# Banded attention and a gated MLP in one kernel: the plain units' scores and sink products take all 128 rows of the array

## The chip, the cores and the metric

One core of a Trainium2 chip runs the whole program. The metric is the device time of one execution in microseconds (us), as the median of several runs. TensorE (PE) multiplies, VectorE (DVE), ScalarE (ACT) and GpSimd (POOL) do the elementwise work, SyncE (SP) issues every DMA. PEld in a profile is TensorE's weight load, which may run beside a product.

## The reference, cut to what matters

```
# q, k, v: [4, 8, 768, 64]; n_sink = 4, window = 128 (read on the chip)
scores = q @ k.T / sqrt(64)
keep   = (col < n_sink) | ((row - col >= 0) & (row - col < window))
a      = softmax(where(keep, scores, -1e9))        # sum + 1e-9 below
x      = (a @ v) -> [3072, 512]                    # heads side by side
out    = (sigmoid(x @ w_gate) * (x @ w_val)) @ w_out     # 512 -> 1536 -> 512
```

Everything is float32.

## The kernel before, in words

**Attention.** The work is cut into units: one head of one stretch of T = 2 tiles (256 tokens); there are 96, numbered u, the heads of a stretch in a row. `attend` (line 719) records the steps of a unit: loads of q, k and v; per tile a product of scores (`qk`), mask and row maximum on DVE (`top`), exponential on ACT (`exp`); the sum's inverse (`guard` and a reciprocal) and the scaling of P on POOL, ACT or DVE; transposes of P on TensorE (`turn`), a copy to `wt`, two triangular selections on POOL (`split`), and the products with v (`pv`), the last of which is that of the sinks, the 16 first tokens' columns. A score tile has 144 columns (its own 128 keys and 16 sinks) or 272 (and the 128 keys before).

**Plain units.** The first 16 units (`PLAIN`, line 31) multiply in float32, which takes four times as many passes; the later ones split their operands into two fp32r halves side by side and then contract over all 128 rows anyway. A plain unit holds q and k turned, head dimension on the rows, in `qkT`, of which only rows 0 to 63 are used; its scores therefore contract over K = D = 64 rows (line 760). The sinks' product contracts over 16 rows: the sinks' v in `VSRAW` and their weights, copied out of PSUM into one buffer `low` (line 887; line 888 is the copy), both at rows 0 to 15 for even heads and 64 to 79 for odd ones (line 923). In a trace these are `a<-qkT 64*128` (rows * columns of the loaded weights) and `a<-low,xr 16*64`; `a<-wt,vraw 128*64` are the products with v.

**MLP.** Tokens are taken in nine chunks. Chunk 0 (`WHOLE = 1`, 2 tiles) multiplies float32 weights as they come, as soon as the first eight units have left their results in `X0` (they lie in buffers named `qs`, `kh`, `kl` and `vhl`): `m<-qs,ws` and its like are its up products, `o<-ws,th` its down products. Weights come in 36 loads of 512 KB into three buffers `wst` and are decoded by ACT, POOL and DVE (`decode`, line 1006). Later chunks multiply fp32r halves (`m<-XH,ws`, `m<-XL,ws`, `o<-ws,gh`).

**What sets the order.** Nothing is issued as it is written. Each step is given to a planner (`Plan`, line 256) with a priority, a duration for each engine that can do it, and what it reads and writes. `Plan.run` plays the steps through in a model of time, picks for each engine the ready step of lowest priority, chooses an engine where there are several, gives out buffers, and writes down one fixed order for each engine. At times when TensorE would stand idle in that model, before 130 us, it adds a filler, a product of the identity with itself (`warm`, `m<-ident` in a trace), so that TensorE stays active. The model counts a plain unit's scores as half activity (`busy=0.5`, line 781). All engines then run their fixed orders and wait for each other by semaphores. Since all steps are recorded by one helper, line 489 stands in nearly all rows of the trace.

Of the kernel before, what the change touches and what calls it, by code (L numbers as in the profile page):

```python
# [9 lines left out]
F32 = mybir.dt.float32  # L10
# [10 lines left out]
NS = 16  # L21
# [52 lines left out]
BUFS = {}  # L74
# [157 lines left out]
class Tile:  # L232
# [7 lines left out]
    def __call__(self):  # L240
        if isinstance(self.pool, list):
            return self.pool[self.slot]
        if self.got is None:
            name = f"{self.tag}{self.slot}"
            self.got = self.pool.tile(self.shape, self.dtype, tag=name, name=name, bufs=1)
        return self.got


# [187 lines left out]
def kernel(  # L436
# [17 lines left out]
    B, H, D, S = q.shape  # L454
    DM, DF, _ = w_gate.shape
# [5 lines left out]
    KW = 128 + NS  # L461
# [6 lines left out]
    p1 = main.enter_context(tc.tile_pool(name="p1", bufs=1))  # L468
# [10 lines left out]
    plan = Plan()  # L479

    class InOrder:


        def __init__(self, engine):
            self.engine = engine
# [5 lines left out]
    PE, V, A, G, Q = (  # L491
        InOrder(e) for e in (nc.tensor, nc.vector, nc.scalar, nc.gpsimd, nc.sync)
    )
# [10 lines left out]
    def mac(cols):  # L504
        return max(cols * 13 / 12 / 2.4, 104.5) + 2.5

    def dma(prio, ns, fn, r=(), w=()):
        plan.op(prio, [("Q", 460, fn)], r, w, dma=ns)

    def copy(prio, cols, out, in_, r, w, psum=False):  # L510

        plan.op(
            prio,
            [
                ("A", act(cols, psum), lambda: A.copy(out=out(), in_=in_())),
                ("V", vec(cols, not psum), lambda: V.tensor_copy(out=out(), in_=in_())),
            ],
            r, w,
        )
# [23 lines left out]
    class Fixed:  # L543
# [5 lines left out]
        def __call__(self):  # L549
            return self.tile  # L550

    def tile(shape, dtype, tag, bufs, pool=None):
        return Tile(pool or p1, shape, dtype, tag, bufs)
# [5 lines left out]
    VSRAW = tile([128, H // 2, D], F32, "xr", BUFS["xr"])  # L559
# [115 lines left out]
    chunk_of = [i for i, parts in enumerate(MT) for _ in range(sum(parts))]  # L675
    X0 = {}

    def sinks(b, u):
        if not b:
            for o in (0, 64):  # L680
                dma(
                    u, 91.0, lambda o=o: Q.dma_start(
                        out=VSRAW()[o : o + NS],
                        in_=v[b, o // 64 :: 2, 0:NS, :].rearrange("h p d -> p h d"),
                    ), w=[(VSRAW, o)],
                )
        raw = tile([128, H, D], F32, "wst", BUFS["wst"], p2)
        u = max(u, PLAIN) + SINKP
        for o in range(0, 128, NS):
            dma(  # L690
                u, 91.0, lambda o=o: Q.dma_start(
                    out=raw()[o : o + NS], in_=v[b, :, 0:NS, :].rearrange("h p d -> p h d"),
                ), w=[(raw, o)],
            )
        for i in range(2):
            hs = slice(i * H // 2, i * H // 2 + H // 2)
            x, hi = lambda hs=hs: raw()[:, hs], lambda hs=hs: VSHL()[:, hs, 0:D]
            copy(u, H // 2 * D, hi, x, [raw], [(VSHL, i)])
            rest(u, H // 2 * D, lambda hs=hs: VSHL()[:, hs, D : 2 * D], x, hi, [raw], [(VSHL, i)])

    def load(u, b, h, t0, T, prev, L, vraw, qkT, plain):

        W, k0 = T * 128, (t0 - prev) * 128
        for part, src, o, n in ((0, k, (t0 - prev) * KW, L * KW), (2, q, t0 * 128, W)):
            at = 0 if part else W
            for i in range(1 if plain else 2):
                dma(
                    u, 0.75 * n, lambda i=i, src=src, o=o, n=n, at=at: Q.dma_start(
                        out=qkT()[i * D : i * D + D, at : at + n],
                        in_=src[b, h, :, o : o + n],  # L710
                    ), w=[(qkT, part + 4 * i)],
                )
        dma(
            u, 182.0 * L, lambda: Q.dma_start(
                out=vraw(), in_=v[b, h, k0 : k0 + L * 128].rearrange("(l p) d -> p l d", p=128)
            ), w=[vraw],
        )

    def attend(u, b, h, t0, T, XR):

        prev = 1 if t0 else 0
        L = T + prev
        W = T * 128
# [2 lines left out]
            sinks(b, u)  # L726
        plain = u < PLAIN
        vraw = tile([128, L, D], F32, "vraw", BUFS["vraw"])
        qkT = tile([128, W + L * KW], F32, "qkT", BUFS["turned"])
        qT = lambda: qkT()[:, 0:W]  # L730
        kTf = lambda: qkT()[:, W : W + L * KW]
        load(u, b, h, t0, T, prev, L, vraw, qkT, plain)
        kk2, qq2 = [(qkT, 0), (qkT, 4)], [(qkT, 2), (qkT, 6)]
        if plain:
            pairs = ((qT, kTf),)
            qk_reads, qk_ns = [qkT], 4
        else:
# [10 lines left out]
            pairs = (qs, kh), (qs, kl)  # L748
# [4 lines left out]
        for t in range(T):  # L753
            sc = tile([128, 512], F32, "a", BUFS["a"], ps)
            first = t0 + t == 0
            n = KW if first else KW + 128

            def qk(t=t, sc=sc, n=n):
                s0 = max(t + prev - 1, 0) * KW
                K = D if plain else 128  # L760
                for i, (qq, kk) in enumerate(pairs):
                    PE.matmul(
                        sc()[:, 0:n], lhsT=qq()[0:K, t * 128 : t * 128 + 128],
                        rhs=kk()[0:K, s0 : s0 + n], start=i == 0, stop=i == len(pairs) - 1,
                    )

            def top(t=t, sc=sc, first=first):
                if not first:
                    V.copy_predicated(out=sc()[:, 0:128], mask=tri, data=sc()[:, KW : KW + 128])
                V.tensor_tensor_reduce(  # L770
                    out=P()[:, t], in0=sc()[:, 0:KW], in1=am[min(t0 + t, 2)], op0=ALU.add,
                    op1=ALU.min, scale=-SCALE, scalar=3.0e38, accum_out=negm_all[:, u, t : t + 1],
                )

            def exp(t=t):
                A.activation(
                    out=P()[:, t], in_=P()[:, t], func=AF.Exp, bias=negm_all[:, u, t : t + 1],
                    scale=-1.0, accum_out=rs()[:, t : t + 1],
                )

            plan.op(u, [("PE", 10 + qk_ns * mac(n), qk)], qk_reads, [sc, (P, t)], busy=0.5 if plain else 0.9)
            plan.op(
                u, [("V", 290 if first else 600, top)],
                [sc, (MASKS, 3), (MASKS, min(t0 + t, 2))], [sc, (P, t)],
            )
            plan.op(u, [("A", 460, exp)], [], [(P, t), (rs, t)])
# [28 lines left out]
        if not plain:  # L815
            st = tile([128, T, 2, NS], F32R, "st", BUFS["st"])
            turned = tile([128, T, 2 * NS], F32, "turned", BUFS["st"])
            sk = tile([128, T, 4, 32], F32R, "sk", BUFS["sk"])
# [23 lines left out]
        w = lambda: wt()[:, 0:Z]  # L842
# [41 lines left out]
        o = 64 * (h % 2)  # L884
        if plain:
            vhl = vraw
            sk = tile([128, W], F32, "low", BUFS["small"])
            copy(u, W, lambda: sk()[o : o + NS], lambda: tp()[0:NS, W : 2 * W], [tp], [sk], True)
        else:
            vhl = tile([128, L, 2 * D], F32R, "vhl", BUFS["vhl"])  # L890
            copy(u, L * D, lambda: vhl()[:, :, 0:D], vraw, [vraw], [(vhl, 0)])
            rest(
                u, L * D, lambda: vhl()[:, :, D : 2 * D], vraw, lambda: vhl()[:, :, 0:D],
                [vraw, (vhl, 0)], [(vhl, 1)],
            )
# [9 lines left out]
        for l in range(L):  # L905
            tl = l - prev
            n = 128 if (tl < 0 or tl == T - 1) else 256
# [6 lines left out]
        def pv():  # L914
            a = (xr()[e : e + D] if plain else acc())[:, 0 : Z * W].rearrange("p (z x) -> p z x", z=Z)
            for i, (_, l, c0, r0, n) in enumerate(blocks):
                PE.matmul(
                    a[:, :, c0 : c0 + n], lhsT=vhl()[:, l],
                    rhs=w().rearrange("p z t x y -> p z (t x y)")[:, :, r0 : r0 + n],
                    start=i == 0, stop=False, skip_group_check=True,  # L920
                )
            if plain:
                sv, sw = VSRAW()[o : o + NS, h // 2], sk()[o : o + NS]
            else:
                sv, sw = VSHL()[:, h], sk().rearrange("p t x y -> p (t x y)")
            PE.matmul(
                a[:, 0], lhsT=sv, rhs=sw, start=False, stop=True, skip_group_check=True
            )
# [7 lines left out]
        else:  # L936
            low = tile([D, W], F32, "low", BUFS["small"])
# [32 lines left out]
        if h % 2:  # L970
# [8 lines left out]
            for run in runs:  # L979
# [3 lines left out]
                x = lambda cols=cols: xr()[:, cols]  # L983
# [237 lines left out]
    u = g = fed = ci = 0  # L1221
    for b in range(B):
        t0 = 0
        for T in AT[b]:
# [6 lines left out]
            while ci < len(MT) and fed + sum(MT[ci]) <= g:  # L1231
                feed(ci, fed, MT[ci])
                fed += sum(MT[ci])
                ci += 1
    plan.run(WARM, 245.0, warm)
    wres = {f: [w() if i < 4 else w()[:, 0] for i, w in enumerate(ws)] for f, ws in wres.items()}


# [64 lines left out]
```

## Time and profile before

| | |
|---|---|
| median of 3 runs | 822.87 us (820.37 to 824.41) |
| the profiled execution | 821.27 us |
| its span in the trace | 819.3 us |
| TensorE busy | 801.7 us, 98% |
| VectorE busy | 529.1 us, 65% |
| ScalarE busy | 420.1 us, 51% |
| GpSimd busy | 470.0 us, 57% |
| mean granted TensorE clock | 0.988 of full speed |

The span runs from the first to the last recorded instruction; 2.0 us of the execution lie around it. Busy time is the time covered by an engine's instructions. The granted clock is a share of 2.4 GHz; 0.50 is 1.2 GHz. A stretch with a clock between these two holds both. A float32 product shows as two records ("x2"), since it runs in two halves with a weight load each.

### The profile page before, as it was taken

The page shows a single profiled execution, that of the slowest core. Times are in us where ns is not written, and L with a number is a line of the kernel's source. Part 1 is how long each engine was busy: PE and PEld are TensorE (multiplying, and loading weights), DVE is VectorE, ACT ScalarE, POOL GpSimd, SP SyncE. Part 2 cuts the span into 40 slices and gives each one's busy share as a digit, 9 for nine tenths or more (in the row PEclk, how much of TensorE's full clock was granted, in tenths as well). Part 3 has the DMA queues.
Part 4 walks back from the last instruction along what each step waited for, and adds up shares of the span by engine and source line. Part 5 has one row for each costly group of instructions (what it writes and reads, how often), then busy time and mean ns, then how long its engine had stood idle before and what let it go on. Part 6 is the DMA issues. An engine that isn't in the chain of part 4 may idle for free.

```text
span 819.3 us, 14819 instructions
## 1 busy us (share of the span) xinstructions
PE 801.7 (98%) x4472; PEld 706.3 (86%) x4472; DVE 529.1 (65%) x1659; ACT 420.1 (51%) x1232; POOL 470.0 (57%) x666
## 2 busy tenths in 40 slices
PE   7999999999999999999999999999999999999997
PEld 5666576789999999999899988899899999999996
DVE  4668787988888888786951499956961495111111
ACT  4667777766677777654730377734640373001001
POOL 3467788787777777664851488755751474111111
PEclk7899999999999999999999999999999999999999
DMA  5567796454454553334341243433441141112112
GB/s 166 152 175 231 206 275 205 110 149 126 130 157 119 144 130 94 107 105 116 103 113 40 66 137 86 134 100 97 104 119 38 50 109 27 48 34 88 40 38 68
DMA packets 101013, 92.93 MB, mean 113 GB/s; under 512 B 47680, under 2 KB 82496, under 8 KB 100928
## 3 DMA queue, kind: packets, MB, share of 16 engines
q1 hardware_dynamic: 100928, 91.93, 40.4%
q8 instruction: 38, 0.62, 0.3%
q14 instruction: 47, 0.39, 0.1%
HBM read 82.45 MB, written 9.44 MB: 112 GB/s over the span
## 4 chain that ended last, share of the span: by engine, by line
PE 67%; DVE 8%; POOL 2%; ACT 2%; DMA 1%; issue 1%; SPq 0%; POOLq 0%; DVEq 0%; ACTq 0%
PE m L489 39%; PE o L489 19%; PE a L489 9%; DVE rs L489 1%; DMA qkT<-in_k_dram 1%; DVE P L489 1%; DVE st L489 1%; DVE gl L489 1%; POOL kl L489 1%; DVE xr L489 1%; DVE a L489 1%; ACT P L489 1%; DVE low L489 1%; DVE th L489 0%; POOL wt L489 0%
## 5 line engine op out<-in xcount | busy, mean ns | idle before, releaser
L489 PE MATMUL m<-XH,ws 128*128 128x384 f32 (+1 forms) x1536 | 399.7, 325 | 0.2 <-DVE th L489 0.2
L489 PEld LDWEIGHTS m<-XH,ws 128*128 128x128 f32 x1536 | 273.9, 188 | 2.9 <-DVE th L489 0.4
L489 PE MATMUL m<-XL,ws 128*128 128x384 f32 (+1 forms) x768 | 247.6, 322 | 0.0
L489 DVE SCALAR_TENSOR_TENSOR th<-th,m 128x384 f32<-128x384 f32 (+1 forms) x108 | 54.6, 505 | 193.5 <-PE m L489 190.3
L489 POOL TENSOR_TENSOR gl<-th,gh 128x384 fp32r<-128x384 f32 (+1 forms) x61 | 61.4, 1006 | 188.9 <-DVE gh L489 183.5
L489 ACT ACTIVATE th<-m 128x384 f32<-128x384 f32 (+1 forms) x108 | 49.1, 455 | 222.5 <-PE m L489 221.5
L489 PEld LDWEIGHTS m<-XL,ws 128*128 128x128 f32 x768 | 144.9, 189 | 2.5
L489 POOL TENSOR_SCALAR_AFFINE_SELECT wt<-wt 128x512 fp32r<-128x512 f32 (+3 forms) x192 | 121.1, 631 | 33.4 <-DVE wt L489 13.7
L489 PE MATMUL o<-ws,gh 128*128 128x512 f32 x264 | 106.4, 403 | 0.0
L489 PE MATMUL o<-ws,gl 128*128 128x512 f32 x264 | 104.3, 395 | 0.7 <-DVE gl L489 0.4
L489 PE MATMUL o<-wol,gh 128*128 128x512 f32 x264 | 103.2, 391 | 0.0
L489 ACT ACTIVATE P<-P,negm_all 128x144 f32<-128x144 f32 x192 | 78.9, 411 | 29.5 <-DVE negm_all L489 24.3
L489 DVE CUSTOM_DVE_ANT_0 P<-a,am 128x144 f32<-128x144 f32 x192 | 58.3, 305 | 7.9 <-PE a L489 2.2
L489 PEld LDWEIGHTS o<-ws,gl 128*128 128x128 f32 x264 | 49.5, 188 | 14.6 <-DVE gl L489 1.8
L489 ACT ACTIVATE P<-P,rs 128x144 f32<-128x144 f32 x114 | 44.1, 410 | 22.5 <-DVE rs L489 22.1
L489 PEld LDWEIGHTS o<-wol,gh 128*128 128x128 f32 x264 | 49.7, 188 | 5.7
L489 PEld LDWEIGHTS o<-ws,gh 128*128 128x128 f32 x264 | 49.7, 188 | 5.2
L489 POOL TENSOR_TENSOR qs<-qkT,qs 64x256 fp32r<-64x256 f32 x57 | 44.4, 779 | 16.0 <-issue 4.5
L489 POOL TENSOR_TENSOR kl<-qkT,kh 128x432 fp32r<-128x432 f32 (+1 forms) x45 | 50.1, 1112 | 3.9 <-ACT kh L489 2.0
L489 PE MATMUL a<-wt,vhl 128*128 128x256 f32 (+1 forms) x216 | 49.2, 330 | 0.5 <-POOL wt L489 0.3
L489 DVE COPY_PREDICATED a<-tri,a 128x128 f32<-128x128 int32 x160 | 45.4, 284 | 6.2 <-PE a L489 5.5
L489 PE MATMUL a<-kh,qs 128*128 128x272 f32 (+1 forms) x160 | 46.5, 295 | 1.1 <-DVE wt L489 0.5
(129 smaller groups left out, 1460.2 us busy)
## 6 DMA issues: line engine op xcount, KB each, us to landing
wol<-wol_d SPq DMA_DIRECT2D x96, 256.0 KB, 2.8
qkT<-in_k_dram SPq DMA_DIRECT2D x120, 108.0 KB, 2.7
qkT<-in_q_dram SPq DMA_DIRECT2D x176, 64.0 KB, 2.4
wst<-in_moe_w_gate_dram SPq DMA_DIRECT2D x12, 512.0 KB, 4.4
wst<-in_moe_w_val_dram SPq DMA_DIRECT2D x12, 512.0 KB, 4.1
wst<-in_moe_w_out_dram SPq DMA_DIRECT2D x12, 512.0 KB, 4.6
vraw<-in_v_dram SPq DMA_DIRECT2D x64, 96.0 KB, 2.3
out_dram<-w SPq DMA_DIRECT2D x23, 256.0 KB, 2.3
```

Source lines behind the costliest of these rows:

```text
L489: return lambda *a, **kw: tc.keep_in_program_order(op(*a, **kw))
```

## The change: what it does

Scores and sink products of the plain units now contract over all 128 rows. For that the rows that hold nothing must be zero:

- `qkT` of a plain unit is one of three tiles of fixed size that all 16 units share, by slot (`Shared`); rows 64 to 127 of each are set to zero once, for the first three units. The loads write rows 0 to 63 only, as before.
- `VSRAW` is set to zero as a whole before its two loads.
- The sinks' weights go to two tiles `SK0`, zeroed once, one for even and one for odd heads, in the buffers `sk` that the later units use; before it was the single buffer `low`.
- Each zeroing is a step of the planner, for POOL or DVE, at the priority of its unit.

```diff
+class Shared(Tile):
+    def __init__(self, kept, *args):
+        super().__init__(*args)
+        self.kept = kept
+    def __call__(self):
+        if self.got is None:
+            got = self.kept.get(self.slot)
+            self.got = got if got is not None else super().__call__()
+            self.kept[self.slot] = self.got
+        return self.got
...
+    def zero(prio, tile, ns, ap, part=None):
+        plan.op(
+            prio, [("G", ns, lambda: G.memset(ap(), 0.0)), ("V", ns, lambda: V.memset(ap(), 0.0))],
+            w=[tile if part is None else (tile, part)],
+        )
+    SK0 = [tile([128, 2 * 128], F32, "sk", BUFS["sk"]) for _ in range(2)]
+    HALVES, FIRST = {}, []
     def sinks(b, u):
         if not b:
+            zero(u, VSRAW, 300.0, VSRAW)
+            for x in SK0:
+                zero(u, x, 300.0, x)
...
-        qkT = tile([128, W + L * KW], F32, "qkT", BUFS["turned"])
+        qkT = (
+            Shared(HALVES, p1, [128, 2 * 128 + 3 * KW], F32, "qkT", BUFS["turned"]) if plain
+            else tile([128, W + L * KW], F32, "qkT", BUFS["turned"])
+        )
...
+        if u < BUFS["turned"]:
+            zero(u, qkT, 700.0, lambda: qkT()[D:128], 8)
+            FIRST.append(qkT)
...
-                K = D if plain else 128
                 for i, (qq, kk) in enumerate(pairs):
                     PE.matmul(
-                        sc()[:, 0:n], lhsT=qq()[0:K, t * 128 : t * 128 + 128],
-                        rhs=kk()[0:K, s0 : s0 + n], start=i == 0, stop=i == len(pairs) - 1,
+                        sc()[:, 0:n], lhsT=qq()[:, t * 128 : t * 128 + 128],
+                        rhs=kk()[:, s0 : s0 + n], start=i == 0, stop=i == len(pairs) - 1,
                     )
...
-            sk = tile([128, W], F32, "low", BUFS["small"])
+            sk = SK0[h % 2]
...
-                sv, sw = VSRAW()[o : o + NS, h // 2], sk()[o : o + NS]
+                sv, sw = VSRAW()[:, h // 2], sk()
```

The planner's durations and its `busy=0.5` stand as they were, but with five more buffers' steps and other ready times it writes another order. It differs over the first 1,941 of the 4,431 rows of TensorE's order (equal instructions in a run make one row); after them the two orders are the same, row by row. The fillers are 59 before and 60 now.

On TensorE, behind the scores of the first two units (`a_152` and `a_158` are unit 0's second score tile, `m_91<-ident` the fillers, `a_195` and `a_208` the turned P of unit 0), before and now:

```order
L489 MATMUL a_152<-qkT_114 128x272
L489 MATMUL a_162<-qkT_131 128x144
L489 MATMUL a_169<-qkT_131 128x272
L489 MATMUL m_91<-ident 128x128 x4
L489 MATMUL a_195<-ident,P_154 128x128
```

```order
L504 MATMUL a_158<-qkT_109 128x272
L504 MATMUL a_168<-qkT_120 128x144
L504 MATMUL a_175<-qkT_120 128x272
L504 MATMUL m_91<-ident 128x128 x11
L504 MATMUL a_208<-ident,P_164 128x128
```

Eleven fillers stand where four stood, ahead of unit 0's transposes; what is added here is taken out further on.

On SP, the queue of the loads, ahead of the fourth load of weights (`wst`); before, `qkT` is that of units 3, 4 and, behind the weights, 5; now it is that of units 5 and 6:

```order
L489 DMA qkT_166<-in_k_dram 64x288
L489 DMA qkT_166<-in_q_dram 64x256
L489 DMA qkT_178<-in_k_dram 64x288
L489 DMA qkT_178<-in_q_dram 64x256
L489 DMA wst_227<-in_moe_w_gate_dram 128x4x256
L489 DMA qkT_235<-in_k_dram 64x288
```

```order
L504 DMA qkT_122<-in_k_dram 64x288
L504 DMA qkT_122<-in_q_dram 64x256
L504 DMA qkT_109<-in_k_dram 64x288
L504 DMA qkT_109<-in_q_dram 64x256
L504 DMA wst_266<-in_moe_w_gate_dram 128x4x256
```

The fourth load of weights stood behind the loads of unit 4; now it stands behind those of unit 6, which wait until TensorE has read unit 3's scores out of the same buffer.

## Rows read from the trace of the kernel before

**Rows 1.** The page's first part: busy time of each engine, share of the span, instructions.

```profile
PE 801.7 (98%) x4472; PEld 706.3 (86%) x4472; DVE 529.1 (65%) x1659; ACT 420.1 (51%) x1232; POOL 470.0 (57%) x666
```

**Rows 2.** Busy time of each engine by stretches of the span: the stretch and its length, then each engine's busy us (and instructions), the granted clock, the DMA engines' busy share, GB/s.

```profile
8.50:11.30 2.80, 2.80 (x14) 2.65 (x14) 0.98 (x5) 0.48 (x3) 0.98 (x2) 0.50 0.87 281
...
15.00:28.30 13.30, 12.62 (x40) 7.88 (x39) 5.06 (x18) 6.95 (x19) 6.22 (x9) 0.50 0.59 171
28.30:58.20 29.90, 29.90 (x163) 20.02 (x164) 20.58 (x67) 21.75 (x54) 17.80 (x25) 1.00 0.56 163
58.20:131.20 73.00, 73.00 (x314) 47.80 (x313) 58.06 (x144) 56.72 (x126) 57.24 (x64) 1.00 0.81 231
131.20:165.00 33.80, 30.74 (x159) 23.28 (x158) 31.83 (x73) 24.97 (x64) 28.51 (x33) 1.00 0.52 145
165.00:380.00 215.00, 214.48 (x1400) 201.16 (x1399) 176.76 (x598) 140.58 (x464) 154.89 (x237) 1.00 0.46 123
```

**Rows 3.** The timeline of TensorE from 5 to 31.5 us: start, length, what, records in a run, and idle time before with what ended it. A run takes in the rows of other widths that follow it.

```profile
5.73 0.94 PE L489 MATMUL a<-qkT 64*128 64x144 f32 x4 [0.49 <-DMA qkT<-in_q_dram]
...
8.47 2.07 PE L489 MATMUL m<-ident 128*128 128x128 f32 x8
10.34 1.06 PE L489 MATMUL a<-ident,P 128*128 128x128 f32 x4
11.19 0.55 PE L489 MATMUL m<-ident 128*128 128x128 f32 x2
...
13.84 0.66 PE L489 MATMUL a<-ident,P 128*128 128x128 f32 x4 [1.66 <-POOL P L489]
...
15.92 1.54 PE L489 MATMUL a<-wt,vraw 128*64 128x256 f32 x4 [0.68 <-POOL wt L489]
17.39 1.11 PE L489 MATMUL a<-low,xr 16*64 16x256 f32 x2
18.43 1.22 PE L489 MATMUL m<-ident 128*128 128x128 f32 x4
19.59 1.75 PE L489 MATMUL a<-qkT 64*128 64x144 f32 x4
...
24.93 2.08 PE L489 MATMUL m<-ident 128*128 128x128 f32 x8
...
28.22 1.13 PE L489 MATMUL a<-qkT 64*128 64x144 f32 x4
```

**Rows 4.** The waits of all engines from 15.9 to 28.3 us: who waited for whom, us in total, times, longest.

```profile
POOL rs L489 <- ACT P L489: 5.5, 2, 4.4
ACT qs L489 <- PE a L489: 3.6, 1, 3.6
```

**Rows 5.** The timeline of TensorE from 72.3 to 78.5 us, columns as in rows 3.

```profile
72.44 0.59 PE L489 MATMUL m<-qs,ws 128*128 128x256 f32 x2
72.87 0.59 PE L489 MATMUL m<-kh,ws 128*128 128x256 f32 x2
73.39 1.08 PE L489 MATMUL a<-wt,vraw 128*64 128x256 f32 x6
74.41 0.64 PE L489 MATMUL a<-low,xr 16*64 16x256 f32 x2
74.98 1.18 PE L489 MATMUL a<-qkT 64*128 64x272 f32 x4
76.09 1.98 PE L489 MATMUL o<-ws,th 128*128 128x512 f32 x4
77.91 0.59 PE L489 MATMUL m<-kl,ws 128*128 128x256 f32 x2
```

**Rows 6.** The timeline of TensorE from 64.5 to 69.5 us, columns as in rows 3.

```profile
65.27 1.02 PE L489 MATMUL o<-ws,th 128*128 128x512 f32 x2
66.22 0.72 PE L489 MATMUL a<-qkT 64*128 64x272 f32 x2
66.87 1.13 PE L489 MATMUL o<-ws,th 128*128 128x512 f32 x2
67.84 0.60 PE L489 MATMUL a<-ident,P 128*128 128x128 f32 x4
```

**Rows 7.** TensorE's weight loads in the stretch of rows 6, same columns.

```profile
66.22 0.29 PEld L489 LDWEIGHTS a<-qkT 64*128 64x128 f32 x2 [0.76 <-PE a L489]
```

**Rows 8.** What TensorE waited for from 126 to 166 us, columns as in rows 4.

```profile
PE o L489 <- DVE th L489: 1.6, 2, 1.2
PE a L489 <- POOL kl L489: 0.8, 1, 0.8
```

**Rows 9.** GpSimd's groups of instructions in the first 2.5 us: line, operation, shapes, count, busy us and mean ns, idle time before.

```profile
masks.py:197 POOL MEMSET ident<- 128x128 f32 x1 | 0.2, 205 | 0.3 <-POOLq L1275 0.3
```

**Rows 10.** The timeline of GpSimd from 8.4 to 14 us, columns as in rows 3.

```profile
8.67 0.23 POOL L489 TENSOR_SCALAR rs<-rs 128x2 f32<-128x2 f32 x1 [6.40 <-ACT P L489]
...
13.03 0.75 POOL L489 TENSOR_SCALAR P<-P,rs 128x144 f32<-128x144 f32 x1 [0.30 <-DVE rs L489]
```

**Rows 11.** The timeline of SP's DMA issues in the first 60 us, columns as in rows 3.

```profile
14.99 0.37 SPq L489 DMA_DIRECT2D wst<-in_moe_w_gate_dram  x1
```

**Rows 12.** The timeline of TensorE from 28 to 45 us, columns as in rows 3.

```profile
39.86 0.70 PE L489 MATMUL m<-qs,ws 128*128 128x256 f32 x2
```

**Rows 13.** The timeline of TensorE from 147 to 166 us, columns as in rows 3.

```profile
151.92 0.47 PE L489 MATMUL m<-XH,ws 128*128 128x256 f32 x1
```

More of the change, by code (lines that the diff above doesn't have):

```diff
@@ L1235 @@
     plan.run(WARM, 245.0, warm)
+    assert len({x.slot for x in FIRST}) == BUFS["turned"]
     wres = {f: [w() if i < 4 else w()[:, 0] for i, w in enumerate(ws)] for f, ws in wres.items()}
```

## The prediction

> **What bounds the kernel now.** I read the page's first part first: TensorE is busy for 801.7 us of 819.3, no other engine for more than 65% [rows 1]. So the end comes earlier only where TensorE loses time. Next the table by stretches [rows 2]. From 165 to 380 us TensorE is idle for 0.5 us of 215: what has been gained by 165 us stays. TensorE is without a gap from 28.3 to 131.2 us too. From 131.2 to 165 us it is idle for 3.06 us, while DVE is busy for 31.83 of 33.8: there the others set the pace, and TensorE waits for DVE and POOL [rows 8]. The third thing to see is the clock: 0.50 from 8.5 to 11.3 us and from 15 to 28.3 us, and full from there on.
>
> The timeline of that second stretch [rows 3] shows TensorE working without a gap from 15.92 to 28.22 us, 12.3 us, at half clock: plain products with v, sinks' products over 16 rows, scores over 64 rows, a few fillers. The clock rises only behind the fillers and transposes, all over 128 rows, that stand from 24.93 to 28.22 us. The waits of these microseconds [rows 4] show who suffers: ACT waits 3.6 us for TensorE, and POOL waits 5.5 us for an exponential that comes late for the same reason. In this stretch TensorE's speed sets everyone's.
>
> The last view is TensorE's timeline where the clock is full [rows 5 to 7]. Products over the full array follow each other without loss: 0.43 us from one of 256 columns to the next [rows 5], so 0.46 for 272 columns and 0.86 for 512. A product of scores does not fit in so smoothly: from 65.27 to 67.84 us two products of 512 columns and one of scores take 2.57 us, where 0.86 + 0.46 + 0.86 = 2.18 would do [rows 6]. Its weight load, 64 rows by 128 columns, begins when its product does, after 0.76 us without a load [rows 7]; a load ahead of time would have been hidden.
>
> **What the change removes.** *The clock.* If rows without work keep the clock low, scores over 128 rows and sinks over 128 in place of 16 raise it earlier. The 12.3 us from 15.92 us would be 6.15 at full clock, a gain of at most 6.2; the 2.8 us of the first slow stretch [rows 2] would give 1.4 more. Not all of it can come in: unit 0's products with v still wait for POOL at 15.92 us [rows 3], and behind them each unit passes through ACT, DVE and POOL. The lower end is 0, the clock as it is. I take 5.0, near the upper end, because the others' waits there end on TensorE [rows 4].
>
> The Trainium skill speaks against this term. Its page "TensorE: Matmul & The Clock Gate", Part 1, says that the chip watches how busy the engine has been recently and that sustained matmuls release the clock; rows of the array are not in it, and by it the term would be 0. The trace does not agree with it taken as busy time: 12.3 us without a gap, and the clock rose only at the end of them.
>
> *The place of the scores among full products.* A lone product of scores costs 2.57 - 2.18 = 0.39 us beyond its columns [rows 6]. For a pair: 1.11 us from 74.98 to 76.09 where 0.91 would do, and the two products behind it take 1.82 where 1.72 would, together 0.30 [rows 5]. Over 128 rows a scores' weight load has the shape of those that are hidden. The order now holds 10 lone products and 11 pairs: 10 x 0.39 + 11 x 0.30 = 7.2 us of TensorE's time; the two first pairs stand where TensorE waits for loads (0.49 us ahead of 5.73 [rows 3]), which leaves 6.6. Of these, 4 lone ones and 7 pairs stand ahead of the last filler, 3.7 us, and the rest, 2.9, behind it. I take 1.5 of the first part (between 0 and 3.7), since the fillers show a TensorE that has time there, and 0 of the second (between 0 and 2.9): from 58 us to 165 us a faster TensorE would only meet the others' pace sooner. The sinks' products take 0.57 us where 256 columns need 0.43 [rows 5]; being 64 columns wide they stay outside that shape, and I count nothing (between 0 and 0.14 x 16 = 2.2).
>
> **What it adds.** Six zeroings. The nearest row: POOL sets 128 columns to zero in 0.205 us [rows 9], so 256 columns in some 0.41 and 688 in 1.1. POOL's three take 2.6 us, and it is idle for 6.40 us ahead of 8.67 [rows 10]; they stand there. DVE's three have the same columns and end before unit 2 needs its buffer. The cost is nothing, with POOL's idle time as the cover; without it unit 0's scores would start up to 2.6 us later. Contracting over more rows costs no time: a product over 64 rows takes no less per column than one over 128 [rows 5, 6].
>
> **What it moves.** Eleven fillers stand ahead of unit 0's transposes in place of four. Four take 1.87 us at half clock (8.47 to 10.34), 0.47 each [rows 3]: eleven take 5.2 us at half clock and 2.6 at full. At full clock the transposes start at 11.1 us instead of 10.3, but behind them TensorE waited 1.66 us for unit 1's P anyway [rows 3], which POOL scales at 13.03 [rows 10], so that delay is covered. On SP the fourth load of weights, issued at 14.99 [rows 11], now waits for the loads of unit 6, and with them for unit 3's scores. At full clock these come some 2 us after 14.99; chunk 0 does not need these weights yet. For the rest of the new order I put a loss of 1.0 us in the stretch from 131.2 us, where DVE has 2 us of slack and an earlier TensorE will be idle longer (between -1 and 3).
>
> **The sum.** 821.27 - 5.0 - 1.5 + 1.0 = 815.8 us, made against the profiled execution, which is 1.6 below the median of 822.87. I forecast 816. No change that is under 0.5%, 4.1 us, can be told from none here, so faster means below 818.8 and slower above 827.0.
>
> **The rivals.**
> - *Both terms come in whole.* 6.2 + 1.4 of clock and 6.6 + 2.2 of shapes give up to 16; what the others can follow is less, 9 to 14: 807 to 812. For it: ACT, DVE and POOL are busy for under 75% of the time from 28.3 to 58.2 us [rows 2]. Against: 131 to 165 us, where DVE has no room.
> - *The clock stays.* This is the page's rule: only the shapes are left, 1.5 us, and eleven fillers at half clock take about 1 of it back: 821. For it: nothing shows rows by themselves at work; the fillers at 24.93 us are 128 columns wide as well, and the products with v stay at 64. Against: the gapless stretch at half clock.
> - *The others hold the pace.* The clock rises, but ACT, DVE, POOL and the loads arrive at 165 us when they did before, and TensorE's idle time from 131 us grows by what it gained: 820. For it: DVE's 31.83 of 33.8 us. Against: before 58 us they wait for TensorE.
> - *Slower: the weights start late.* The clock stays, and the eleven fillers end at 8.47 + 5.2 = 13.6 us. Up to unit 3's scores, which the fourth load of weights now waits for, stand two units' transposes (0.85 each, 10.34 to 11.19), two pairs of scores (1.75 each [rows 3]) and three fillers (1.4): 20.2 us, and with unit 6's loads 21. That is 6 us behind 14.99 [rows 11], and the next load is behind unit 1's product with v. If chunk 0 ends on its last weights, 5 of these 6 us may arrive at the end: 826 on the profiled execution, 828 on the median. It decides only if the loads have no slack; the DMA share of 0.56 from 28.3 to 58.2 us [rows 2] says that they have some.
>
> **How the numbers follow.** The forecast, 812 to 818.8, has 0.45; both terms whole 0.14; the clock stays 0.18; the others hold the pace 0.14; slower 0.09. Faster: 0.45 + 0.14 = 0.59. Slower 0.09. The rest, 0.32, is within 0.5%. The range, 807.5 to 823.5, holds the first four cases and leaves out the slower one and the tail of the whole gain. The likeliest case alone is 812 to 818.8.
>
> **What would show it.** Right, step by step: a granted clock of 1.00 from about 11 us on, no stretch at 0.50 from 15 to 28; a lone product of scores that takes 0.46 us between its neighbours, with its load ahead of it; the first chunk products (39.86 us before [rows 12]) some 8 us earlier, and the first of chunk 1 (151.92 us [rows 13]) 5 to 6 us earlier; TensorE's idle time from 131 us at 3 to 5 us. I am wrong in the main step if the clock still stands at 0.50 after 16 us; in the place of the gain if the clock is up and chunk 1 opens less than 3 us earlier; and in the zeroings if unit 0's scores start more than 0.3 us after 5.73 [rows 3].

## The result, and the profile after

The changed kernel takes 808.99 us (median of 4 runs, 807.40 to 810.34), the kernel before 822.81 beside it (820.37 to 824.41): ratio 0.9834, 95% interval 0.9803 to 0.9864. That is 13.8 us less, where 6.9 were forecast: direction and range held, the size did not. The profiled execution took 808.61 us, its span is 806.9.

The page's first part, which answers to [rows 1]:

```profile
PE 788.8 (98%) x4474; PEld 705.8 (87%) x4474; DVE 534.9 (66%) x1666; ACT 420.9 (52%) x1233; POOL 475.5 (59%) x664
```

TensorE is busy for 12.9 us less and the span is 12.4 shorter; its idle time is 18.1 us where it was 17.6. So the net gain is busy time of TensorE. The same stretches as in [rows 2], same columns:

```profile
8.50:11.30 2.80, 2.80 (x28) 2.76 (x27) 1.16 (x6) 0.97 (x5) 0.98 (x2) 1.00 0.93 274
11.30:15.00 3.70, 1.26 (x10) 0.99 (x8) 2.05 (x7) 1.96 (x4) 1.90 (x2) 1.00 1.05 311
15.00:28.30 13.30, 12.45 (x59) 8.56 (x60) 7.80 (x27) 7.23 (x20) 6.37 (x12) 0.74 0.43 120
28.30:58.20 29.90, 28.73 (x168) 21.77 (x167) 26.28 (x72) 24.00 (x61) 23.21 (x28) 1.00 0.71 205
58.20:131.20 73.00, 71.03 (x314) 49.81 (x313) 62.15 (x146) 58.64 (x123) 58.98 (x65) 1.00 0.85 243
131.20:165.00 33.80, 33.11 (x207) 28.52 (x206) 30.07 (x83) 26.32 (x74) 29.00 (x34) 1.00 0.52 141
```

Three things: the first slow stretch is gone (1.00 at 8.5 us), of the second about half is left (0.74), and from 131.2 us, where I expected 3 to 5 us of idle time in place of 3.06, TensorE is idle for 0.69. TensorE's timeline from 8 us on, columns as in rows 3, shows where the clock still falls, and the first chunk products:

```profile
8.36 2.62 PE L504 MATMUL m<-ident 128*128 128x128 f32 x22
10.81 0.60 PE L504 MATMUL a<-ident,P 128*128 128x128 f32 x4
...
15.36 0.66 PE L504 MATMUL a<-ident,P 128*128 128x128 f32 x4 [2.80 <-POOL P L504]
...
16.59 1.73 PE L504 MATMUL a<-qkT 128*128 128x144 f32 x4 [0.34 <-DMA qkT<-in_q_dram]
18.24 1.54 PE L504 MATMUL a<-wt,vraw 128*64 128x256 f32 x4
...
22.63 0.77 PE L504 MATMUL a<-sk,xr 128*64 128x256 f32 x2
23.33 1.16 PE L504 MATMUL m<-ident 128*128 128x128 f32 x8
...
32.03 0.60 PE L504 MATMUL m<-qs,ws 128*128 128x256 f32 x2
```

The eleven fillers take 2.62 us for 22 records, full speed. At 12.56 us TensorE runs dry and waits 2.80 us for unit 1's P. Behind that wait the scores of two tiles take 1.73 us, about the half-speed length of [rows 3] (1.75); the fillers of 23.33 us run at full speed again. The first chunk product starts 7.8 us earlier than [rows 12]. A lone product of scores, and then its weight loads, where [rows 6, 7] showed the old shape:

```profile
55.80 0.59 PE L504 MATMUL a<-sk,xr 128*64 128x256 f32 x2
56.32 0.66 PE L504 MATMUL a<-ident,P 128*128 128x128 f32 x4
56.81 1.02 PE L504 MATMUL o<-ws,th 128*128 128x512 f32 x2
57.67 0.62 PE L504 MATMUL a<-qkT 128*128 128x272 f32 x2
58.13 1.02 PE L504 MATMUL o<-ws,th 128*128 128x512 f32 x2
```

```profile
57.25 0.19 PEld L504 LDWEIGHTS a<-qkT 128*128 128x128 f32 x1 [0.24 <-PE a L504]
57.68 0.19 PEld L504 LDWEIGHTS a<-qkT 128*128 128x128 f32 x1 [0.24 <-issue]
```

From the product of scores to its neighbour are 0.46 us, from the neighbour before to it 0.86: the columns alone, no loss. The load at 57.25 runs ahead of its product. The sinks' products start 0.52 us ahead of the next work (0.57 before). The first product of chunk 1, which answers to [rows 13], is 13.9 us earlier. The end is 12.4 earlier: behind this product TensorE is busy for 659.60 us where it was 657.40, as a little work moved there.

```profile
138.02 0.47 PE L504 MATMUL m<-XH,ws 128*128 128x256 f32 x1
```

Between the first chunk product and this one lie 105.99 us, before 112.06 ([rows 12, 13]). The forecast had the first 8 us and the second 5 to 6 us earlier, and so would have lengthened this stretch; it became 6.1 us shorter.

### The profile page after: what moved, and what is told of

The parts are those of the page before. It is cut to its first block, busy times and chain, and to the rows that moved or that the text cites. A ratio compares the mean times of both kernels' runs of the same rounds, so it can differ in the third digit from the quotient of the medians.

```text
span 806.9 us, 14812 instructions
## 1 busy us (share of the span) xinstructions
PE 788.8 (98%) x4474; PEld 705.8 (87%) x4474; DVE 534.9 (66%) x1666; ACT 420.9 (52%) x1233; POOL 475.5 (59%) x664
## 4 chain that ended last, share of the span: by engine, by line
PE 68%; DVE 12%; DMA 5%; POOL 4%; ACT 3%; issue 2%; SPq 1%; POOLq 0%; DVEq 0%; ACTq 0%
PE m L504 39%; PE o L504 20%; PE a L504 9%; DMA wst<-in_moe_w_out_dram 3%; DVE ws L504 2%; DVE rs L504 1%; DMA wst<-in_moe_w_gate_dram 1%; DVE P L504 1%; ACT ws L504 1%; POOL wst L504 1%; DVE xr L504 1%; DVE gl L504 1%; DVE st L504 1%; POOL wt L504 1%; DVE a L504 1%
## 5 line engine op out<-in xcount | busy, mean ns | idle before, releaser
L504 POOL TENSOR_TENSOR gl<-th,gh 128x384 fp32r<-128x384 f32 (+1 forms) x58 | 57.3, 987 | 188.1 <-DVE gh L504 184.7
L504 POOL TENSOR_TENSOR qs<-qkT,qs 64x256 fp32r<-64x256 f32 x61 | 48.6, 797 | 17.7 <-POOL wt L504 5.4
L504 ACT ACTIVATE P<-P,rs 128x144 f32<-128x144 f32 x125 | 47.3, 409 | 21.5 <-DVE rs L504 19.8
L504 POOL TENSOR_TENSOR kl<-qkT,kh 128x432 fp32r<-128x432 f32 (+1 forms) x49 | 54.7, 1117 | 5.2 <-DVE st L504 1.9
```

What stands on the lines that cost most here:

```text
L504: return lambda *a, **kw: tc.keep_in_program_order(op(*a, **kw))
```

## The experiments

The kernel before ran beside each batch: 822.31, 822.67 and 821.57 us (medians). The reader should follow two numbers for each kernel: the time, and how long TensorE works at half speed ahead of 30 us.

**Which part lifts the clock? Four kernels with part of the change.** First the new order and zeroings with the old rows:

```diff
-                        sc()[:, 0:n], lhsT=qq()[:, t * 128 : t * 128 + 128],
+                        sc()[:, 0:n], lhsT=qq()[0:D, t * 128 : t * 128 + 128],
...
-                sv, sw = VSRAW()[:, h // 2], sk()
+                sv, sw = VSRAW()[o : o + NS, h // 2], sk()[o : o + NS]
```

> The changed kernel's order and zeroing, but scores over 64 rows and sinks' products over 16 again, in all plain units. Theory A (the rows themselves bring the gain: clock and the fit of the products on TensorE): about the kernel before, 820 to 825 us, with a clock of 0.50 again over some 13 us between 15 and 30 us and 0.39 us lost around each lone product of scores. Rival R1 (the new order of the planner brings a large part of it): 811 to 816 us.

Measured 812.90 us (6 runs, 809.04 to 824.15), ratio 0.9898 (0.9856 to 0.9939). Theory A, that the rows bring the whole gain, fell here: with no row added, 9.4 us are gone by the medians, 5 to 12 by the interval. Its windows, columns as above, and the fillers:

```profile
11.30:15.00 3.70, 3.70 (x21) 3.43 (x19) 0.65 (x3) 1.34 (x2) 2.22 (x2) 0.56 0.94 297
15.00:28.30 13.30, 13.30 (x75) 8.85 (x74) 10.33 (x38) 9.77 (x26) 7.86 (x13) 1.00 0.50 134
```

```profile
9.01 5.06 PE L504 MATMUL m<-ident 128*128 128x128 f32 x22
```

The eleven fillers run at half speed (5.06 us), but the clock is up from some 14.4 us on and stays. Its runs scatter, though: the longest two, 818.99 and 824.15 us, have mean clocks of 0.991 and 0.983, the shortest 0.999. Without the longest, which the ratio leaves out, the median is 811.80.

Then the reverse, the order of before with all rows:

```diff
-                K = D if plain else 128
+                K = 128
...
-                sv, sw = VSRAW()[o : o + NS, h // 2], sk()[o : o + NS]
+                sv, sw = VSRAW()[:, h // 2], sk()
+    nc.gpsimd.memset(HALVES[0][D:128], 0.0)   # and four more, once, at the very start
```

> The order of the kernel before, row by row on every engine, with scores and sinks' products over 128 rows; the zeroing stands ahead of all planned work. One buffer serves the sinks' weights of even and odd heads, so that each sinks' product of a plain unit after the first also adds what the unit before left in the other rows: the result differs there, the work does not. Theory A: 808 to 813 us, nearly the whole gain. Rival R1 (the new order brings a large part): 815 to 820 us.

Measured 810.98 (5 runs, 810.21 to 813.24), ratio 0.9866 (0.9841 to 0.9891). This hit theory A's number: the rows, too, bring most of the gain without the new order. With four fillers as before, the granted clock is at 0.50 from 14.7 to 17.4 us alone:

```profile
15.00:28.30 13.30, 13.03 (x80) 9.72 (x79) 9.83 (x34) 11.12 (x28) 9.93 (x15) 0.90 0.74 213
```

So either part by itself brings most of it: 9.4 and 11.3 us, and both together 13.8, not 20.7. They remove the same loss.

Full rows in the first six units only, and in the other ten only (the edit is the condition `u < 6` or `u >= 6` on the rows):

> The changed kernel with full rows in units 0 to 5 only; units 6 to 15 over 64 and 16 rows as before. Theory A, by parts: clock some 6 us and the products' fit in 6 of 16 units, 2 to 3 us: 813 to 816 us, clock as in the changed kernel. Rival R2 (the clock is all of it): 808 to 811 us.

> The changed kernel with full rows in units 6 to 15 only; units 0 to 5 over 64 and 16 rows as before. Theory A, by parts: no gain in the clock, the products' fit in 10 units at some 0.55 us each: 815 to 819 us. Rival R2 (the clock is all of it): 820 to 824 us.

Measured 812.08 (810.83 to 814.11), ratio 0.9875 (0.9849 to 0.9900), and 811.73 (807.81 to 812.64), ratio 0.9864 (0.9836 to 0.9892). Both medians lie between the new order with no full rows and the changed kernel; their intervals overlap with each other and with both of those. Neither theory hit: the first came out between A and R2, the second below both. Both theories took it that the order does not lift the clock, and the kernel with no full rows shows that it does. Where the full rows are worth most stays open.

**Are the fillers what the order does? Two kernels.** The kernel before with seven more fillers behind the first two units' scores, and the new order with old rows and seven of its eleven fillers taken out:

```diff
-        for o, e, fn in order:
-            fn()
+        n, more, drop = 0, {12: 7}, ()     # the second kernel: {} and (13, 14, ..., 19)
+        for o, e, fn in order:
+            if o is None:
+                n += 1
+                for _ in range(0 if n in drop else 1 + more.get(n, 0)):
+                    fn()
+            else:
+                fn()
```

> The kernel before (its order, its rows) with seven more fillers behind the scores of the first two units, eleven in place of four. Theory A2 (the new order gains because its eleven fillers lift the clock early): the clock is up by 15 us and the slow stretch from 15 to 28 us is gone or much shorter, 813 to 818 us. Rival R3 (the new order gains by the other places it gives to loads, copies and products): 820 to 824 us.

> The changed kernel's order with rows as before (64 and 16) and seven of the eleven fillers taken out, so that four stand there. Theory A2: the clock stays at 0.50 from about 8.5 us to 23 us or later, 818 to 823 us. Rival R3: as with the eleven, 811 to 814 us.

Measured 816.24 (12 runs, 814.08 to 824.52), ratio 0.9940 (0.9912 to 0.9968): seven products of the identity with itself make the kernel 6.4 us faster by the medians. They do so in most executions and not in all: nine of the twelve took 814.08 to 817.28 us, with mean clocks of 0.996 to 0.999, the other three 822.09 to 824.52, with 0.988 and 0.989, as the kernel before.

The second kernel takes 820.84 (12 runs, 815.35 to 826.14), ratio 0.9967 (0.9942 to 0.9991): without the seven fillers the new order keeps 1.8 of its 9.4 us. Here, too, three runs stand apart, 815.35 to 816.73 us with mean clocks of 0.990 to 0.999. A2 holds twice by the medians, R3 falls twice. Its windows, from an execution that was the longest of its twelve (826.14 us, mean clock 0.980), and the place where its products become short again:

```profile
15.00:28.30 13.30, 13.25 (x41) 8.54 (x42) 5.73 (x18) 4.98 (x16) 5.28 (x9) 0.50 0.40 108
28.30:58.20 29.90, 29.90 (x128) 19.52 (x126) 15.22 (x54) 17.38 (x45) 15.42 (x21) 0.74 0.50 143
```

```profile
42.42 1.06 PE L510 MATMUL m<-kh,ws 128*128 128x256 f32 x2
...
44.36 0.59 PE L510 MATMUL m<-kh,ws 128*128 128x256 f32 x2
```

TensorE is busy with hardly a gap and still at half clock well beyond 28.3 us. The kernel before with full rows and four fillers was busy for no more of the time (16.01 us from 8.5 to 28.3, here 16.44, in the kernel before 17.46), and its clock was up at 17.4. It differs from the kernel before in the rows and in five zeroings at the very start, and each of its five runs is shorter than every run of the kernel before, so the rows are what lifted the clock there.

The fillers that begin near 8 us say the same. The first line is of the old order with full rows, the second of the new order without the seven fillers:

```profile
8.20 1.05 PE L504 MATMUL m<-ident 128*128 128x128 f32 x8
8.34 1.16 PE L510 MATMUL m<-ident 128*128 128x128 f32 x8
```

In all seven traced kernels whose first two units have scores over 128 rows these fillers run at full speed (1.05 us for 8 records, 2.17 for 18, 2.62 for 22). With 64 rows there are nine traces: in seven the fillers run at half speed for all or most of their length (2.07 us for 8 records, 4.35 to 5.06 for 22), in two at full speed (the second line, and 2.72 us for 22 records with the sinks' rows alone). With 64 rows, then, one execution is not like the next; with 128 rows all seven traces are alike. The Trainium skill, "TensorE: Matmul & The Clock Gate", Part 1, lets sustained matmuls release the clock, with no word of rows; these windows do not agree with that.

**The shapes at full clock. Three kernels.** Scores alone over 128 rows, sinks alone, each with the new order (the edits are one each of the two lines of the first diff):

> The changed kernel with scores over 128 rows and sinks' products over 16 rows, as before. Theory by shapes (a sinks' product and its neighbours lose 0.15 us per unit when its shape differs from that of the products with v): 2 us above the changed kernel, 810.5 to 812 us. Rival (sinks' products stay exposed either way): 808.5 to 810 us.

> The changed kernel, its new order and zeroings, with scores over 64 rows again and sinks' products over 128. Beside the changed kernel (808.99 us) it lacks the scores' shape alone, beside the one with both at their old rows (812.9) it has the sinks' shape alone. Theory S (the shapes add up: some 4 us of scores and 2 of sinks): 810.5 to 812.5. Rival (only the scores' shape counts; what the kernel with scores alone over 128 rows lacked to 808.99 was the scatter of the clock): 812.5 to 814.

Measured 811.11 (6 runs, 808.48 to 813.57), ratio 0.9861 (0.9835 to 0.9886), and 810.47 (6 runs, 808.78 to 812.93), ratio 0.9860 (0.9835 to 0.9886), between 812.90 with neither and 808.99 with both. The theory that the shapes add up expected both about there (the second is 0.03 us below its range). All four intervals overlap, so the share of each is open, and even the 3.9 us of both together are not clear of noise here. In the old order the shapes were measured with eleven fillers on both sides:

> The kernel before, its order kept, with scores and sinks' products over all 128 rows (zeroings at the very start) and with eleven fillers, in place of four, behind the first two units' scores. The one buffer of the sinks' weights serves both kinds of heads, so the sinks' products also add what the other kind left in the other rows. It differs from the kernel with eleven fillers and rows 64 and 16 (816.24 us) in the rows alone, and there the granted clock is full from 14 us on with either. Theory S (the place of the scores among full products is worth what the trace of before shows, 6.6 us and 2.2 for the sinks, and the others follow for most of it): 809 to 812. Theory F, my forecast's step (1.5 us come in, the others hold the pace behind 58 us): 814 to 816.

Measured 811.57 (6 runs, 808.60 to 815.58), ratio 0.9883 (0.9857 to 0.9910), against 816.24, ratio 0.9940: 4.7 us for the rows alone, and the intervals do not overlap. Theory S, near its upper end; theory F, the step of my forecast, falls.

How much of this is the shapes at full clock? The first chunk products of three kernels, the new order with old rows, the old order with eleven fillers and old rows, and the same with full rows:

```profile
30.55 0.60 PE L504 MATMUL m<-qs,ws 128*128 128x256 f32 x2
35.18 0.70 PE L495 MATMUL m<-qs,ws 128*128 128x256 f32 x2
33.03 0.59 PE L510 MATMUL m<-qs,ws 128*128 128x256 f32 x2
```

From here to the end the two kernels of one order have the same work on TensorE, at a recorded clock of 1.00 or close to it. In the new order this takes 779.25 us with old rows and 774.87 with full ones; in the old order 779.22 and 773.77. That is 4.4 and 5.5 us, of 6.0 by which TensorE's busy time falls there in each pair. With four fillers the old order takes 779.44 and, with full rows, 776.89: 2.6 us. One trace shows none of it: the changed kernel with twelve more fillers (below), in the longest of its runs, opens at 29.41 us and then takes 779.49. These are single executions, so a size for the shapes alone is not settled; three of four lie above the 1.5 us of my forecast. Of the 4.7 us, some stand ahead of the first chunk product (35.18 and 33.03 us), where the eleven fillers run at half speed with old rows (5.05 us) and at full speed with full ones (2.62): this part is clock.

Beside 810.98 with four fillers, the 811.57 also show that with full rows the seven extra ones buy nothing.

**Is there more to get? Two kernels.** Twelve more fillers in the wait of 2.80 us at 12.56 us, so that the clock never falls (the loop of the fillers above, in the changed kernel):

```diff
-        n, more, drop = 0, {12: 7}, ()
+        n, more, drop = 0, {21: 12}, ()
```

> The changed kernel with twelve more fillers in the 2.8 us in which TensorE waits for unit 1's P. Theory A2: the clock does not fall at 16.6 us any more, which spares up to 3 us: 805 to 807.5 us. Rival (the others hold the pace there): 808 to 810 us, with the clock up.

Measured 807.78 (5 runs, 806.40 to 810.68), ratio 0.9814 (0.9792 to 0.9836), between the two expectations. By the lengths of its products the clock is full from 8.2 us on, the first chunk product is 2.6 us earlier than in the changed kernel, at 29.41, and yet:

```profile
11.98 3.06 PE L510 MATMUL m<-ident 128*128 128x128 f32 x26
```

```profile
58.20:131.20 73.00, 69.08 (x301) 47.54 (x299) 57.13 (x136) 56.09 (x118) 54.45 (x62) 1.00 0.79 229
131.20:165.00 33.80, 32.16 (x202) 27.57 (x201) 29.61 (x82) 26.03 (x72) 29.41 (x33) 1.00 0.57 155
```

From 58.2 to 165 us TensorE is now idle for 5.56 us, in the changed kernel for 2.66: the others hold the pace. It is the lowest median of all, but its interval overlaps that of the changed kernel, so it is not shown to beat it. The last one gives the planner the activity 0.9 for plain scores, `busy=0.9` in place of `0.5 if plain else 0.9`:

> The changed kernel with the planner's activity of a plain unit's scores at 0.9 in place of 0.5, which is what the other products over 128 rows have there. The planner writes another order, nine fillers behind the first two units' scores in place of eleven, and the others elsewhere. Theory A3 (full rows alone keep the clock up, the fillers are spent for nothing, and the end does not move): 806 to 811. Rival (the clock falls back to 0.50 for over 10 us for lack of fillers): 814 to 820.

Measured 810.38 (5 runs, 808.75 to 811.05), ratio 0.9859 (0.9834 to 0.9883). Its interval overlaps that of the changed kernel: twelve fillers fewer make no difference that can be seen, and the clock does not collapse (0.50 from 15 to some 18.4 us). Theory A3 holds.

**Does the kernel before always lose this time? Three more profiles of it.** Of its 45 runs beside the three batches (the first text below says 38, a miscount), 12 had a mean clock of 0.998 or 0.999 and were no shorter.

> The kernel before, unchanged, for its trace: of its 38 runs so far whose clock is listed, 12 show a mean granted clock of 0.998 or 0.999 and are no shorter (819.7 to 826.7 us) than those at 0.985 to 0.989. Theory M (the records of the clock miss a slow stretch in such runs, as in the kernel with eleven fillers, whose fillers took twice their time at a recorded 1.00): where the mean is 0.998 or more, TensorE's products still take twice their time from 15.9 to 28 us, and the first chunk products stand near 39.9 us. Rival (the clock is full there and the time is lost elsewhere): scores of two units in 0.95 us in place of 1.75 behind 16 us, first chunk products at 34 to 36 us.

> The same kernel once more, with the same two expectations: theory M, first chunk products near 39.9 us whatever the recorded clock; rival, at 34 to 36 us where the recorded clock is 0.998 or more.

> The same kernel a third time, with the same two expectations: theory M, first chunk products near 39.9 us whatever the recorded clock; rival, at 34 to 36 us where the recorded clock is 0.998 or more.

Measured 821.74 (mean clock 0.998), 825.27 (0.998) and 820.35 us (0.989). The first of them, a window and its timeline:

```profile
15.00:28.30 13.30, 13.30 (x41) 8.22 (x42) 5.08 (x18) 6.83 (x18) 6.17 (x9) 1.00 0.55 170
```

```profile
16.02 1.54 PE L489 MATMUL a<-wt,vraw 128*64 128x256 f32 x4
17.48 1.11 PE L489 MATMUL a<-low,xr 16*64 16x256 f32 x2
...
19.68 1.75 PE L489 MATMUL a<-qkT 64*128 64x144 f32 x4
```

The window says 1.00, but the lengths are those of [rows 3] to the last digit, 1.54, 1.11, 1.75: half speed. The first chunk products start at 39.59, 42.78 and 39.81 us. Theory M, even beyond its 39.9 in the second: the record missed the slow stretch, the loss was there. So the kernel with eleven fillers too must be read by its products. It shows 1.00 from 8.5 us on, but its fillers run at half speed, and the products from 13.94 on at full:

```profile
9.08 5.05 PE L495 MATMUL m<-ident 128*128 128x128 f32 x22
13.94 0.64 PE L495 MATMUL a<-ident,P 128*128 128x128 f32 x4
```

## Why the prediction was right in direction and wrong in size

**The clock: near in size, wrong on what lifts it.** I took 5.0 us. The half-clock time fell from 16.1 us to 6.3 (16.6 to 22.9 us), which is 4.9 us of TensorE's time. Seven fillers that lift the clock in the old order bring 6.4 us by the medians, although they run at half speed themselves (0.46 us each). In the two traces nearly all of the difference lies ahead of the first chunk product (39.86 and 35.18 us); from there to the end they take the same time (779.44 and 779.22). What I may have missed is that a slow TensorE also makes itself wait: the idle time of the whole span is 17.6 us in the kernel before and 17.8 in the new order without the fillers, both slow, and 14.5 and 13.7 us in the same two orders with the clock up; these are single executions, and no run separates this cause. I was wrong on what lifts the clock. "Eleven fillers in place of four" stood in my text as a cost to be covered; in most executions they are enough by themselves, and so are the rows. And I had written that a clock at 0.50 after 16 us would make the main step wrong: it does stand there, for 6.3 us, behind the 2.80 us wait in which POOL decodes weights (13.00 to 14.57) ahead of unit 1's P. That wait I had put at 1.66 as before. The first chunk products 8 us earlier: 7.8.

**The shape of the products: this step failed in its size.** The prices per product were right: 0.46 us for a lone one, as forecast, loads ahead of time, 0.05 us per sinks' product. From the kernel with the new order and old rows to the changed one TensorE's busy time falls from 796.1 to 788.8 us, 7.3, where my rows gave 6.6 + 2.2, with the half-clock time nearly the same (6.6 and 6.3 us). Then I let in only 1.5 of it, "0 of the second part", because "from 58 us to 165 us a faster TensorE would only meet the others' pace sooner". This is the step that failed. The rows alone, in the order of before, bring 11.3 us (9.0 to 13.1 by the interval), where my two terms for them gave 6.5. With the fillers equal, the rows are worth 4.7 us in the old order by the medians (an estimate from the two intervals: 1.5 to 7.9), and behind the first chunk product alone 2.6 to 5.5 us come in, in three of four pairs of traces. The others took less than I thought. Idle time does rise by 4.4 us between the two kernels of the new order, but 2.8 of that stand ahead of the first chunk product, where TensorE waits for unit 1's P, and 1.6 behind it.

**The new order's loss of 1.0 us in the stretch from 131.2 us: it did not come.** I expected TensorE to be idle there for 3 to 5 us; it is 0.69, and 0.68 with the old rows:

```profile
131.20:165.00 33.80, 33.12 (x203) 27.96 (x202) 32.41 (x83) 26.73 (x73) 30.14 (x35) 1.00 0.55 152
```

With eleven fillers on both sides, the new order is 3.3 us shorter than the old one with the old rows (816.24 to 812.90), 2.6 with all rows (811.57 to 808.99). Both pairs of intervals overlap, and the two traces with all rows have equal spans (806.8 and 806.9 us), so a gain of the order beside its fillers is not shown; which of its moves would bring it was not separated.

**The sum.** Along one path of medians: fillers 6.4, rows 4.7, order 2.6, together 13.7 of 13.8; the first two are clear of noise, the third is not, and the 4.7 hold some clock beside the shapes. Forecast: 5.0, 1.5 and -1.0, together 5.5. The miss of 8.2 is 3.6 of order, 3.2 of shapes and 1.4 of clock; against the median it is 6.9, since the sum was made against an execution 1.6 below it. The two large ones go back to one reading: I took DVE's 31.83 of 33.8 us [rows 2] for a wall. The line above has DVE busier, 32.41 us, and TensorE idle for 0.68 us only.

**What held at no cost.** The zeroings: unit 0's scores start at 5.81 us (5.73 before), and POOL, which zeroes for 1.70 us in two rows, is then idle for 4.60 ahead of its next step:

```profile
1.59 0.31 POOL L504 MEMSET sk<- 128x256 f32 x1
1.96 1.39 POOL L504 MEMSET qkT<- 64x688 f32 x2
...
8.65 0.23 POOL L504 TENSOR_SCALAR rs<-rs 128x2 f32<-128x2 f32 x1 [4.60 <-ACT P L504]
```

The fourth load of weights is issued at 19.91, not at some 17: 4.9 us behind [rows 11], as the slower rival wanted it. It decided nothing; the first chunk products came early all the same.

**The rivals.** "Both terms come in whole" (807 to 812, a chance of 0.14) has the measured time in its range, but the shapes came in for more than I took and not whole. "The clock stays" fell with the first window. "The others hold the pace" is true only behind the change: the kernel with no slow clock at all gains next to nothing more.

## What to carry to other kernels

An engine that is busy for 94% of a stretch need not be a wall: ask what it does once it is fed earlier. Here TensorE's idle time beside it went from 3.06 to 0.69 us. When two parts of a change can remove the same loss, run each alone; here 9.4 and 11.3 us made 13.8. When single runs of a kernel stand apart, look at each run's clock before trusting the median. A small product that loads 64 rows among full ones costs more than its columns say (0.39 us for a lone one here): look in the timeline for weight loads that begin with their product.

## What the runs showed of the hardware

- The recorded clock can miss a slow stretch: two of three further profiles of the kernel before say 1.00 where products take twice their full-speed time (1.75 us in place of 0.97 for two tiles' scores over 64 rows). Lengths of like products are the surer reading.
- Eleven products over the whole array, 128 columns each, ran at half clock (5.05 us) and were followed by the full one; by the times and the mean clocks this happened in nine of twelve executions. In the new order without seven of them the engine worked with hardly a gap at 0.50 from 15 to some 43 us, with products of 64 and 16 rows among them.
- With full rows in all plain units the clock, once up, fell behind a wait (2.80 us in the changed kernel, 2.74 with the old order), and came back after 6.3 and 2.7 us.
- The time scatters more where 64 rows leave the clock to chance: over 15.1 and 10.4 us in the two kernels with old rows and eleven fillers (6 and 12 runs), over 2.9 in the changed one (4 runs), 3.0 and 7.0 in the old order with full rows (5 and 6 runs). The numbers of runs differ, so this is a hint.
- A lone float32 product of scores among full ones lost 0.39 us with 64 rows, its weight load beginning with it, and nothing with 128, the load running ahead.
